# Retention plus mixture-of-experts on one core: sixteen second products for a fifth tile of at most 64 tokens, low rows put together by VectorE and added by a scatter, other orders of y buffers and of GpSimd's gathers

## The chip, the cores and the metric

The kernel runs on one core of a Trainium2 chip. The metric is the device time of one execution in microseconds (us). TensorE (PE) multiplies; its weight loads are listed apart as PEld. VectorE is DVE, ScalarE is ACT, GpSimd is POOL, and SP issues most of the plain transfers.

## The reference, cut to what matters

```
scores = scale * q @ k^T;  ret = scores * D          # D[h,i,j] = gamma_h^(i-j) for i >= j, else 0
x = (ret @ v) as rows of 512 for 4608 tokens          # 8 batches x 576 positions, 8 heads x 64
idx, gate = argmax and softmax weight of the cosine logits of x with 8 expert rows, / tau
for e in range(8):
    mask = idx == e
    h = max(x[mask] @ w1[e], 0)                        # 512 -> 1024
    out[mask] = gate[mask] * (h @ w2[e])               # 1024 -> 512
```

Every token goes to exactly one of eight experts. Sizes are float32 throughout.

## The kernel before, in words

The first 171 us compute the retention, route the tokens and do the first products of expert 0. The rest is a loop over the eight experts (lines 1416 to 1436), and all of the change lies there or in tables built ahead of it. The order of instructions on each engine is the order in which the code is written; no scheduler moves them.

**Slots.** Each expert has CT = 5 tiles of 128 slots. A token of rank r in its expert takes slot r. Within a tile, slots are dealt out so that even ranks lie on partitions 0 to 63 and odd ranks on 64 to 127 (`route_onehot`, line 294), so the first 64 tokens of a tile fill partitions 0 to 31 and 64 to 95. The tables `gid` (token to read, 0 for an empty slot) and `sid` (row to write, a number beyond the bounds for an empty slot) have one column for each tile. `left` holds for each expert how many tokens lie beyond four tiles, at least 0 (`count_left`, line 487), and PE reads it into registers as `rest[e]`.

**First products** (`product`, line 1210): 28 steps for each expert from 1 on, in the order of `ORDER`, of six matrix products each. They use a seven-product scheme over halves, in which the number of moving columns is 320, 304 or 288 by `rest[e]` (over 96, over 64, the rest). After each step, `follow` has ACT copy a bank into one of the five buffers `ys` (line 1249), DVE add another bank to it (line 1245), and ACT and DVE write the two parts of the hidden rows, `hs[:, 0]` (high) and `hs[:, 1]` (low remainder), at lines 1194 and 1187. `ya`, `yb` and `yc` are the buffers; `yb` for i = 0 to 3 is `ys` 2, 3, 4, 2.

**Second products** (`mm2`, line 1291): for each of the five tiles 24 matrix products of 128 slots by 512 columns of w2: high hs with high w2, high hs with low w2, low hs with high w2, for eight slices of F. ACT scales the bank by the gate into `ys[i]` (line 1315), and POOL issues a scatter of its rows to `out` (line 1277). For the fifth tile of experts 1 to 6 PE jumps over the 24 products when `rest[e]` is 0 (line 1300).

**Tasks.** Between these, `run_tasks` writes the preparation of the next expert into the engines' streams: `mm2_plan` has numbered places 3i + k for part k of tile i, `mm1_plan` one place for each of the 28 steps. `gather` (POOL) fetches the rows of a tile; `xturn` (ACT copy at line 404, then a transposing transfer on SP) turns them, `xjoin`, `xsums`, `xhigh`, `xlow` split them; `w1sum`, `w1hi`, `w1lo` split w1; `gather_gates` (POOL) fetches gate values. In `mm2_plan(e)` these prepare expert e + 1, with gathers for e + 2; `w1lo` of w1 part 1 is the last thing of place 9.

Lines 1299 to 1309 hold the second products, cut:

```
last = i == CT - 1 and 0 < e < NE - 1
with tc.If(rest[e] > 0) if last else nullcontext():
    for j, f in enumerate(SECOND):
        for k, (hsp, ws) in enumerate(((0, 0), (0, 1), (1, 0))):
            nc.tensor.matmul(ps[:, :step], hs[:, hsp, f, i * P : (i + 1) * P], w[:, ws, f, n : n + step], ...)
```

## Time and profile before

| what | us |
|---|---|
| median of 3 runs (lowest, highest) | 560.64 (558.1, 561.66) |
| the profiled execution's own time | 554.6 |
| its span, first to last instruction | 552.8 |
| retention, routing and first products of expert 0 | 171.8 |
| second products of the eight experts, first to last | 171.8 to 548 |
| second products of expert 2 / 3 / 4 | 27.2 / 27.2 / 22.3 |

The profiled execution is 6 us shorter than the median of the timed runs. A sum over its rows is therefore made against 554.6 us, and a difference is then taken over to the median. In the rows further down, times are us from the span's start; a bracket behind a row is the idle time of the engine just before it and what ended it.

### The profile page before, as it was taken

How to read it: one execution, taken by the hardware profiler on the slowest of the kernel's cores; microseconds unless marked ns; L12 is line 12 of the kernel's file. 1: busy time of each engine (PE TensorE's matmuls, PEld its weight loads, DVE VectorE, ACT ScalarE, POOL GpSimd, SP SyncE). 2: the span in 40 equal slices, each digit the busy share in tenths (PEclk: the TensorE clock that was granted, in tenths of full speed). 3: DMA queues.
4: the chain of work that ended last, by engine and by line, in shares of the span. 5: the costliest groups of instructions: out<-in, count | busy, mean ns of one | idle time of the engine just before them, and what ended most of it. 6: DMA issues, size and time to landing. Idle time of an engine off the chain costs nothing. (4 is left out here: it accounts for less than half of the span.)

```text
span 552.8 us, 13528 instructions
## 1 busy us (share of the span) xinstructions
PE 544.5 (98%) x5067; PEld 491.3 (89%) x5067; DVE 417.2 (75%) x939; ACT 375.8 (68%) x700; POOL 240.2 (43%) x233
## 2 busy tenths in 40 slices
PE   8999999999999999999999999999999999999996
PEld 8898988898898899889988988998898899889986
DVE  4856778789875967986896789589978948976810
ACT  1256454457767959967895898589879858957511
POOL 6674435543463661265056207603730750343022
PEclk9999999999999999999999999999999999999999
DMA  9999999968459555847765765557567558641211
GB/s 316 390 392 377 376 319 357 377 254 287 149 195 195 169 184 135 170 145 171 156 179 169 148 154 172 171 158 156 177 172 154 171 173 149 159 133 54 77 39 50
DMA packets 81109, 109.57 MB, mean 198 GB/s; under 512 B 42327, under 2 KB 43771, under 8 KB 81024
## 3 DMA queue, kind: packets, MB, share of 16 engines
q1 hardware_dynamic: 71920, 86.24, 54.1%
q0 software_dynamic: 7696, 19.95, 10.8%
q10 hardware_dynamic: 1408, 2.17, 1.2%
q8 instruction: 62, 1.02, 0.8%
q14 instruction: 23, 0.19, 0.1%
HBM read 80.27 MB, written 19.94 MB: 181 GB/s over the span
## 5 line engine op out<-in xcount | busy, mean ns | idle before, releaser
L1303 PE MATMUL m<-w2s,hs 128*128 128x512 f32 x600 | 138.1, 389 | 0.0
L1303 PEld LDWEIGHTS m<-w2s,hs 128*128 128x128 f32 x600 | 112.4, 188 | 23.2
L1277 POOL DMA_INDIRECT out<-y,sid x41 | 50.3, 1227 | 178.9 <-DVE raw L422 122.7
L1303 PE MATMUL a<-w2s,hs 128*128 128x512 f32 (+1 forms) x360 | 78.8, 375 | 0.0
L1303 PEld LDWEIGHTS a<-w2s,hs 128*128 128x128 f32 x360 | 64.2, 188 | 11.9
L363 POOL DMA_INDIRECT raw<-xd,gid x40 | 44.0, 1101 | 29.4 <-ACT xsb L446 11.8
L376 POOL DMA_INDIRECT gt<-gd,gid x40 | 43.9, 1098 | 19.1 <-issue 12.0
L1187 DVE SCALAR_TENSOR_TENSOR hs<-y,hs 128x320 fp32r<-128x320 f32 x84 | 43.8, 528 | 7.6 <-ACT hs L1194 5.6
L411 ACT COPY raw<-raw 128x1024 uint16<-128x1024 uint16 x35 | 47.9, 1367 | 0.8 <-DMA raw<-raw 0.8
L1194 ACT ACTIVATE hs<-y 128x320 fp32r<-128x320 f32 x84 | 39.4, 476 | 12.6 <-DVE y L1245 11.8
L705 POOL TENSOR_TENSOR kt<-kt,cs 128x512 f32<-128x512 f32 x28 | 28.3, 1042 | 44.9 <-DMA kt<-kn 44.9
L1245 DVE TENSOR_TENSOR y<-a,y 128x320 f32<-128x320 f32 x53 | 25.4, 485 | 29.6 <-ACT y L1249 29.2
L1122 DVE TENSOR_TENSOR w2s<-raw,w2s 128x1024 fp32r<-128x1024 f32 x32 | 39.1, 1221 | 8.4 <-ACT w2s L1119 8.3
L1225 PE MATMUL m<-xsb,w0s 128*128 128x288 f32 (+2 forms) x270 | 43.6, 300 | 0.2
L1225 PE MATMUL a<-xsb,w0s 128*128 128x288 f32 (+2 forms) x270 | 43.2, 300 | 0.0
L1315 ACT ACTIVATE y<-m,gt 128x512 f32<-128x512 f32 x26 | 18.0, 691 | 34.3 <-PE m L1303 34.3
L1225 PEld LDWEIGHTS m<-xsb,w0s 128*128 128x128 f32 x270 | 38.8, 188 | 0.6 <-ACT y L1249 0.6
L1225 PEld LDWEIGHTS a<-xsb,w0s 128*128 128x128 f32 x270 | 38.9, 188 | 0.1
L404 ACT COPY raw<-raw 128x1024 uint16<-128x1024 uint16 x35 | 36.7, 1048 | 0.0
L1119 ACT CAST w2s<-raw 128x1024 fp32r<-128x1024 f32 x32 | 33.4, 1043 | 2.9 <-DMA raw<-w 2.9
L724 POOL TENSOR_TENSOR qkt<-qkt,gsb 128x384 f32<-128x384 f32 x32 | 31.3, 1005 | 5.6 <-issue 3.4
L450 DVE TENSOR_TENSOR xsb<-raw,xsb 128x128 fp32r<-128x128 f32 x70 | 30.5, 483 | 0.0
(259 smaller groups left out, 1177.9 us busy)
## 6 DMA issues: line engine op xcount, KB each, us to landing
raw<-w SPq DMA_DIRECT2D x64, 512.0 KB, 4.0
qkt<-qk SPq DMA_DIRECT2D x28, 576.0 KB, 7.4
xd<-y SPq DMA_DIRECT2D x36, 256.0 KB, 9.4
vt<-vs SPq DMA_DIRECT2D x7, 1152.0 KB, 13.0
kt<-kn SPq DMA_DIRECT2D x7, 1024.0 KB, 10.5
qkt<-qk ACTq DMA_DIRECT2D x4, 288.0 KB, 5.5
qkt<-qk SPq DMA_DIRECT2D x4, 288.0 KB, 5.5
out<-y,sid POOLq DMA_INDIRECT x41, 3.4
```

Source lines behind the costliest of these rows:

```text
L363: nc.gpsimd.indirect_dma_start(out=t[:, XO : XO + DM], out_offset=None, in_=xd[:rows, :], in_offset=bass.IndirectOffsetOnAxis(ap=gid[:, a ...
L376: nc.gpsimd.indirect_dma_start(out=g[:, i : i + 1], out_offset=None, in_=gd[:, :], in_offset=bass.IndirectOffsetOnAxis(ap=gid[:, a : a + 1 ...
L404: nc.scalar.copy(far.rearrange("p (h n) -> p h n", h=2), near.rearrange("p (n h) -> p h n", h=2))
L411: nc.scalar.copy(far.bitcast(U16).rearrange("p (n h) -> p h n", h=2), near.rearrange("p (h n) -> p h n", h=2))
L724: nc.gpsimd.tensor_tensor(out=q, in0=q, in1=gsb[:, p, :], op=ALU.mult)
L1119: nc.scalar.copy(hi, u)
L1122: nc.vector.tensor_tensor(out=lo, in0=u, in1=hi.bitcast(F32), op=ALU.subtract)
L1187: nc.vector.scalar_tensor_tensor(out=lo, in0=part(src), scalar=0.0, in1=hi.bitcast(F32), op0=ALU.max, op1=ALU.subtract)
L1194: nc.scalar.activation(hi, part(src), AF.Relu)
L1225: nc.tensor.matmul(ps[:, :n_cols], w[:, ws, ka, d * P : (d + 1) * P], xop(kx, xsp)[:, d, :n_cols], start=(n in (1, 2, 5) and d == 0 and k ...
L1277: put = nc.gpsimd.indirect_dma_start(out=out.rearrange("t (k n) -> (t k) n", k=k), out_offset=bass.IndirectOffsetOnAxis(ap=rows, axis=0), ...
L1303: nc.tensor.matmul(ps[:, :step], hs[:, hsp, f, i * P : (i + 1) * P], w[:, ws, f, n : n + step], start=(j == 0 and k == 0), stop=(j == NF - ...
```

## The change

For the fifth tile of experts 1 to 6 PE now has three ways: 24 products as before when `rest[e]` is over 64, 16 products when it is 1 to 64, none when it is 0. The 16 products use a tile `ht` in which the high rows of the tile's first 64 slots and their low rows stand beside each other as 128 rows: partitions of the product 0 to 31 and 64 to 95 are high, 32 to 63 and 96 to 127 low. With w2 high and w2 low as the two moving operands they give two rows of y for each token.

`both_parts` has DVE put `ht` together with four copies of 128 x 256 elements out of `hs`, into two pieces of `w0s` that held nothing; it stands in place 9 of `mm2_plan`, for every expert from 1 to 6, whatever its count. The first scatter writes the high rows as before. `add_low` issues a second scatter of the same buffer, `ys[4]`, that adds the low rows to them; it is written after step 10 of the next expert's first products and waits for the first scatter. Its rows come from `sidx`, and the gates of the fifth tile from `gidx`; `low_rows` computes both tables once, with 11 small DVE instructions, and `count_left` one more (`few`). When `few` is 0 for an expert, `sidx` holds rows beyond the bounds.

Moved besides: `xturn(n, 0)` goes from step 8 of the first products to place 12 of the second products before them; `gather` of tiles 2 and 3 goes one place later; `gather_gates` goes in three calls in place of four; `yb` for i = 0 to 3 is `ys` 2, 3, 2, 4.

The diff, cut:

```diff
@@ gather_gates
+            ids = gidx[:, e : e + 1] if fitted(e, i) else gid[:, a : a + 1]
-                in_offset=bass.IndirectOffsetOnAxis(ap=gid[:, a : a + 1], axis=0),
+                in_offset=bass.IndirectOffsetOnAxis(ap=ids, axis=0),
...
+    def low_rows():
+        q = P // 4
+        g, r = tab[:, 0, :NE], tab[:, 1, :NE]
+        nc.vector.memset(r, BIG)
+        nc.vector.tensor_copy(g, fifth(gid))
+        for k in (0, 2):
+            to, of = slice((k + 1) * q, (k + 2) * q), slice(k * q, (k + 1) * q)
+            nc.vector.tensor_copy(g[to], fifth(gid)[of])
+            nc.vector.tensor_copy(r[to], fifth(sid)[of])
...
+        ht = [w0s[:, o : o + NPR * P].rearrange("p (f c) -> p f c", f=NPR) for o in (28 * P, 4096 + 28 * P)]
...
-            ya, yb, yc = ys[min(i, 1)], ys[2 + i % 3], ys[0]
+            ya, yb, yc = ys[min(i, 1)], ys[(2, 3, 2, 4)[i]], ys[0]
...
+        def both_parts():
+            for k in range(2):
+                for o, v in enumerate(ht):
+                    t = hs[:, k, NPR * o : NPR * (o + 1), (CT - 1) * P :].rearrange("p f (h c) -> p f h c", h=2)
+                    v = v.rearrange("p f (h s c) -> p f h s c", h=2, s=2)
+                    nc.vector.tensor_copy(v[:, :, :, k, :], t[:, :, :, : HB // 2])
+        def add_low(e):
+            put_rows(ys[CT - 1], 1, sidx[:, e : e + 1], firsts[e])
...
+                if fitted(e, i):
+                    with tc.If(rest[e] > HB) as many:
+                        passes(three)
+                    with many.Else():
+                        with tc.If(rest[e] > 0):
+                            passes(((ht, 0), (ht, 1)))
...
-                    plan[(2, 4, 7, 8, 11)[i]].append((gather, n + 1, i))
-            for k, a0, a1 in ((2, 0, 2), (5, 2, 3), (8, 3, 4), (11, 4, CT)):
+                    plan[(2, 4, 8, 9, 11)[i]].append((gather, n + 1, i))
+            if fitted(e, CT - 1):
+                plan[9].insert(1, (both_parts,))
+            for k, a0, a1 in ((2, 0, 2), (5, 2, 4), (9, 4, CT)):
                 plan[k].insert(0, (gather_gates, n, a0, a1))
+            if n + 1 < NE:
+                plan[12].append((xturn, n + 1, 0))
...
-                plan[8] = [(xturn, n, 0)]
...
+                    if k == 10 and fitted(e - 1, CT - 1):
+                        add_low(e - 1)
```

What this does to three engines follows, in rows of the order in which instructions stand (line numbers are each kernel's own; `waits` names the engines or queues whose semaphores the instruction waits for).

PE at the end of the second products of expert 2, from the fourth tile on; `m_69` and `m_68` are banks. Before:

```order
L1303 MATMUL m_69<-w2s,hs 128x512 x24
L1300 COMPARE_AND_BRANCH
L1303 MATMUL m_68<-w2s,hs 128x512 x24
L1300 UNCONDITIONAL_BRANCH
L1300 UNCONDITIONAL_BRANCH [waits PE_49]
L1234 COMPARE_AND_BRANCH
```

And now:

```order
L1349 MATMUL m_69<-w2s,hs 128x512 x24
L1366 COMPARE_AND_BRANCH
L1349 MATMUL m_68<-w2s,hs 128x512 x24
L1366 UNCONDITIONAL_BRANCH
L1369 COMPARE_AND_BRANCH
L1349 MATMUL m_68<-w2s,w0s 128x512 [waits DVE_49]
L1349 MATMUL m_68<-w2s,w0s 128x512
L1349 MATMUL m_68<-w2s,w0s 128x512 [waits DVE_49]
L1349 MATMUL m_68<-w2s,w0s 128x512 x13
L1369 UNCONDITIONAL_BRANCH
L1369 UNCONDITIONAL_BRANCH [waits PE_49]
L1264 COMPARE_AND_BRANCH
```

The way of 16 products waits for DVE twice, at its first and its third product; the way of none keeps its wait for PE's own work.

DVE in the second products of expert 2, around the end of place 9; `raw_82` holds the rows of tile 4 of expert 3, `wsum` sums of w1. Before:

```order
L450 TENSOR_TENSOR xsb<-raw_82,xsb 128x2x64 [waits Activation_49]
L450 TENSOR_TENSOR xsb<-raw_82,xsb 128x4x2x64 [waits Activation_49]
L1122 TENSOR_TENSOR wsa<-wsum,wsa 128x1024 [waits Activation_49]
L1145 TENSOR_TENSOR wsum<-raw_83 128x256 [waits DMAHW0_49,DVE_49]
L1145 TENSOR_TENSOR wsum<-raw_83 128x256
```

And now:

```order
L454 TENSOR_TENSOR xsb<-raw_82,xsb 128x2x64 [waits Activation_49]
L454 TENSOR_TENSOR xsb<-raw_82,xsb 128x4x2x64 [waits Activation_49]
L1331 COPY w0s<-hs 128x8x32 x4
L1152 TENSOR_TENSOR wsa<-wsum,wsa 128x1024 [waits Activation_49]
L1366 UNCONDITIONAL_BRANCH
```

The four copies stand behind all of the split of x and ahead of the split of w1.

ACT from the last two tiles of the second products of expert 1 to step 9 of the first products of expert 2; `raw_78` holds the rows of tile 0 of expert 3, and `y_84` to `y_88` are the five buffers `ys`. Before:

```order
L1119 CAST wsa<-raw_83 128x768 [waits DMAHW3_49]
L1315 ACTIVATE y_88<-a_64,gt 128x512 [waits DMASW3_49,PE_49]
L1249 COPY y_84<-a_66 128x320 [waits DMASW6_49,PE_49]
...
L1249 COPY y_84<-a_66 128x320 [waits PE_49,Activation_49]
L404 COPY raw_78<-raw_78 128x1024 [waits DMASW1_49]
L1234 UNCONDITIONAL_BRANCH x2
L1249 COPY y_87<-a_65 128x320 [waits DMASW1_49,PE_49]
```

And now:

```order
L1149 CAST wsa<-raw_83 128x768 [waits DMAHW3_49]
L408 COPY raw_78<-raw_78 128x1024 [waits DMASW1_49]
L1375 ACTIVATE y_88<-a_64,gt 128x512 [waits PE_49]
L1279 COPY y_84<-a_66 128x320 [waits DMASW6_49,PE_49]
...
L1279 COPY y_84<-a_66 128x320 [waits PE_49,Activation_49]
L1279 COPY y_87<-a_65 128x320 [waits DMASW2_49,PE_49]
```

The copy of `xturn` leaves the stretch of first products and stands ahead of the scaling of the fifth tile.

## Rows read from the trace of the kernel before

**Rows 1.** The page: busy us (share) xinstructions; granted clock in 40 slices.

```profile
PE 544.5 (98%) x5067; PEld 491.3 (89%) x5067; DVE 417.2 (75%) x939; ACT 375.8 (68%) x700; POOL 240.2 (43%) x233
PEclk9999999999999999999999999999999999999999
```

**Rows 2.** Timeline of PE: start, us, line, operands, shape, count [idle before].

```profile
199.02 1.86 PE L1225 MATMUL a<-xsa,wsa 128*128 128x304 f32 x12
...
249.58 1.76 PE L1225 MATMUL a<-xsa,w0s 128*128 128x288 f32 x12
...
272.22 11.07 PE L1303 MATMUL a<-w2s,hs 128*128 128x512 f32 x48
283.13 16.48 PE L1303 MATMUL m<-w2s,hs 128*128 128x512 f32 x72
299.45 1.76 PE L1225 MATMUL a<-xsa,w0s 128*128 128x288 f32 x12
...
349.32 1.75 PE L1225 MATMUL a<-xsa,wsa 128*128 128x288 f32 x12
...
388.26 5.60 PE L1303 MATMUL m<-w2s,hs 128*128 128x512 f32 x24
394.18 2.02 PE L1225 MATMUL a<-xsa,w0s 128*128 128x320 f32 x12 [0.32 <-PEq L1300]
```

**Rows 3.** Busy time by stretch: stretch, length, then PE, PEld, DVE, ACT, POOL, clock.

```profile
249.58:272.22 22.64, 22.59 (x170) 22.29 (x168) 16.80 (x28) 19.21 (x36) 7.09 (x7) 1.00 0.70 159
272.22:299.45 27.23, 27.23 (x123) 22.54 (x121) 23.66 (x55) 21.39 (x35) 14.00 (x12) 1.00 0.67 162
```

**Rows 4.** Waits of PE's weight loads: us in total, times, longest.

```profile
PEld m L1225 <- ACT y L1249: 1.3, 4, 0.4
```

**Rows 5.** Timeline of DVE in the second products of expert 2.

```profile
277.96 0.29 DVE L429 TENSOR_TENSOR raw<-raw 128x128 f32<-128x128 f32 x1
278.17 0.42 DVE L450 TENSOR_TENSOR xsa<-raw,xsa 128x256 fp32r<-128x256 f32 x1
278.50 0.75 DVE L1145 TENSOR_TENSOR wsum<-raw 128x256 f32<-128x256 f32 x2
...
293.62 1.21 DVE L1122 TENSOR_TENSOR wsa<-wsum,wsa 128x1024 fp32r<-128x1024 f32 x1
...
301.30 0.49 DVE L1245 TENSOR_TENSOR y<-a,y 128x320 f32<-128x320 f32 x1 [3.95 <-ACT y L1249]
```

**Rows 6.** Timeline of ACT in the first products of expert 2.

```profile
256.52 1.05 ACT L404 COPY raw<-raw 128x1024 uint16<-128x1024 uint16 x1
...
260.46 0.45 ACT L1249 COPY y<-a 128x320 f32<-128x320 f32 x1
...
261.48 0.47 ACT L1194 ACTIVATE hs<-y 128x320 fp32r<-128x320 f32 x1 [0.19 <-DVE y L1245]
...
264.42 0.42 ACT L1249 COPY y<-m 128x320 f32<-128x320 f32 x1
```

**Rows 7.** Timeline of ACT: end of expert 2's second products; first products of expert 5.

```profile
294.80 0.82 ACT L1119 CAST w0s<-raw 128x768 fp32r<-128x768 f32 x1
299.65 0.69 ACT L1315 ACTIVATE y<-m,gt 128x512 f32<-128x512 f32 x1 [4.03 <-PE m L1303]
...
403.86 0.43 ACT L1249 COPY y<-m 128x320 f32<-128x320 f32 x1 [0.92 <-DMA out<-y,sid]
```

**Rows 8.** Timeline of DVE around line 491, at the end of expert 0's first products.

```profile
173.66 0.16 DVE L491 TENSOR_SCALAR left<-a 128x8 int32<-128x8 f32 x1
174.54 0.42 DVE L1167 SCALAR_TENSOR_TENSOR hs<-m,hs 128x256 fp32r<-128x256 f32 x1 [0.72 <-ACT hs L1166]
176.72 0.43 DVE L422 TENSOR_TENSOR raw<-raw 128x256 f32<-128x256 f32 x1 [1.76 <-ACT raw L411]
```

**Rows 9.** POOL's timeline in expert 3's first products; scatters of line 1277, issue to landing.

```profile
308.84 0.88 POOL L1145 TENSOR_TENSOR wsum<-raw,wsum 128x256 f32<-128x256 f32 x1
...
DMA to landing us min/median/max: 2.2/3.4/6.1
```

More of the change, by code (lines that the diff above doesn't have):

```diff
@@ L358, in retention_moe, with fitted @@
     BEG = group_tiles(B - 3)[0] * P
+    def fitted(e, i):
+        return i == CT - 1 and 0 < e < NE - 1
     def gather(e, i, rows=N):
@@ L484, in retention_moe, with fifth @@
     left = keep.tile([P, NE], I32, name="left")
+    few = tab[:, 0, NE : 2 * NE]
+    gidx = keep.tile([P, NE], I32, name="gidx")
+    sidx = keep.tile([P, NE], I32, name="sidx")
     rest = []
+    def fifth(t):
+        return t.rearrange("p (e i) -> p e i", i=CT)[:, :, CT - 1]
+    def low_rows():
[7 more added lines that the diff above has]
+            nc.vector.tensor_copy(r[to], fifth(sid)[of])
+        nc.vector.tensor_tensor(out=g, in0=g, in1=fifth(gid), op=ALU.subtract)
+        nc.vector.tensor_tensor(out=g, in0=g, in1=few, op=ALU.mult)
+        nc.vector.tensor_tensor(out=gidx, in0=g, in1=fifth(gid), op=ALU.add)
+        nc.vector.scalar_tensor_tensor(out=r, in0=r, scalar=-BIG, in1=few, op0=ALU.add, op1=ALU.mult)
+        nc.vector.tensor_scalar(out=sidx, in0=r, scalar1=BIG, scalar2=None, op0=ALU.add)
     def count_left():
@@ L1274, in retention_moe, with put_rows @@
         puts = []
-        def put_rows(rows_of_y, k, rows):
+        firsts = {}
+        def put_rows(rows_of_y, k, rows, first=None):
             put = nc.gpsimd.indirect_dma_start(
@@ L1283, in put_rows @@
                 oob_is_err=False,
+                compute_op=ALU.add if first else ALU.bypass,
             )
             for other in puts:
-                tc.declare_no_dep(put.ins, other.ins, reason="a scatter writes other rows or other columns")
+                if other is not first:
+                    tc.declare_no_dep(put.ins, other.ins, reason="a scatter writes other rows or other columns")
             puts.append(put)
+            return put
         last_rows = []
+        def both_parts():
[6 more added lines that the diff above has]
+            put_rows(ys[CT - 1], 1, sidx[:, e : e + 1], firsts[e])
         def mm2(e, i, tasks):
@@ L1298, in mm2, with passes, between @@
                 ps = psm.tile([P, 512], F32, name="m")
-                last = i == CT - 1 and 0 < e < NE - 1
-                with tc.If(rest[e] > 0) if last else nullcontext():
+                def passes(forms, inner=lambda m: None):
+                    m = 0
                     for j, f in enumerate(SECOND):
-                        for k, (hsp, ws) in enumerate(((0, 0), (0, 1), (1, 0))):
+                        for rows, ws in forms:
                             nc.tensor.matmul(
                                 ps[:, :step],
-                                hs[:, hsp, f, i * P : (i + 1) * P],
+                                rows[f // NPR][:, f % NPR] if rows is ht else rows[:, f],
                                 w[:, ws, f, n : n + step],
-                                start=(j == 0 and k == 0),
-                                stop=(j == NF - 1 and k == 2),
-                            )
-                            if not last and step == DM and (3 * j + k) % 8 == 7 and 3 * j + k < 23:
-                                tasks((3 * j + k) // 8)
-                if last:
+                                start=(m == 0),
+                                stop=(m == NF * len(forms) - 1),
+                            )
+                            m += 1
+                            inner(m)
+                def between(m):
+                    if step == DM and m in (8, 16):
+                        tasks(m // 8 - 1)
+                hi, lo = (hs[:, k, :, i * P : (i + 1) * P] for k in range(2))
+                three = ((hi, 0), (hi, 1), (lo, 0))
+                if fitted(e, i):
[4 more added lines that the diff above has]
+                            passes(((ht, 0), (ht, 1)))
                     tasks(0)
                     tasks(1)
+                else:
+                    passes(three, between)
                 nc.scalar.activation(y[:, n : n + step], ps[:, :step], AF.Copy, scale=gts[e][:, i : i + 1])
@@ L1320, in mm2 @@
                 if a < NA - 2:
-                    put_rows(*part)
+                    firsts[e] = put_rows(*part)
                 else:
@@ L1408, in retention_moe @@
             13: [(xturn, 1, 2)],
-            14: [(count_left,), (xturn, 1, 3)],
+            14: [(count_left,), (low_rows,), (xturn, 1, 3)],
         }
```

3 lines of the change are left out of this document (added).

## The prediction

> **What bounds the kernel now.** I read the page first: the line of busy times and the line of the granted clock. [...]
>
> Second, PE's timeline, to see how full it is and which experts the change touches. The second products of expert 2 run from 272.22 to 299.45 without a gap; 48 products take 10.91 us, 0.227 us each, and a tile of 24 takes 5.45. The stage of first products tells the count of each expert by its columns: 288 for experts 2, 3 and 4, which is at most 64 in the fifth tile; 304 or 320 for experts 1, 5, 6 and 7 (rows of expert 1 and 5 stand for them). After expert 4 one group of 24 follows the fourth tile's place directly by first products: four tiles only, so its fifth is jumped over already [rows 2]. **Only experts 2 and 3 can take the way of 16.**
>
> Third, busy time by stretch: in the second products of expert 2 DVE is busy 23.66 of 27.23 us and ACT 21.39, in its first products 16.80 and 19.21 of 22.64 [rows 3]. Fourth, the waits: the only one of PE in the expert loop that repeats is that of its weight loads for ACT's copy of a bank, 1.3 us in four times [rows 4]. Last, the timelines of DVE, ACT and POOL at the places where the change puts something.
>
> **The products.** Two experts save 8 products of 0.227 us: 2 x 1.82 = -3.64 us [rows 2]. Experts 1, 5 and 6 keep 24, expert 4 keeps none.
>
> **The copies for `ht`.** They cover two of the three possible ways for nothing, but on the way of 16 PE waits for them, and they come late. In expert 2 the instruction behind which place 9's split of x ends, and ahead of which the copies now stand, begins at 293.62 [rows 5]; DVE has little idle time before it, and nothing ahead of it in the order is moved. The fifth tile begins at 283.13 + 48 x 0.227 = 294.0 [rows 2]. The first product needs the first and the third copy. No row shows a copy from SBUF to SBUF of this size on DVE. From above I bound it by a TENSOR_TENSOR of 128 x 256, 0.42 us long with the next one 0.33 later; from below by one of 128 x 128, 0.29 long with the next 0.21 later [rows 5]. The third copy then ends at 293.62 + 2 x 0.33 + 0.42 = 294.70, or at 294.33. How long PE takes to start again I read after expert 4: the last group ends at 388.26 + 5.60 = 393.86 and the next product starts at 394.18, 0.32 later [rows 2]. So PE starts the fifth tile at 294.65 to 295.02 in place of 294.0: it waits 0.65 to 1.0 us. The fourth copy is 0.2 to 0.3 behind the third, within the two products that go first. Nothing excludes that DVE comes earlier than in this trace, so the lower end is no wait at all. I take 0.8 in each of two experts: +1.6 us (0 to 2.0). **Almost half of what is saved goes into this wait.**
>
> [...]
>
> What the copies delay: each expert's split of w1, its sums and a second split, by at most 4 x 0.33 = 1.3 us. After them DVE is idle 3.95 us until the first products [rows 5], so this costs nothing while that idle time is there; on the way of 16 the first products come 1 us sooner, which it still covers. After expert 4, where the fifth tile is missing, it is not there, and I come back to that.
>
> **The moved `xturn`.** PE's four waits for ACT [rows 4] come at step 20 in experts 2 to 5: the product accumulates on a bank that ACT still has to copy. In expert 2 that copy runs from 264.42 to 264.84. ACT has been working almost without idle time from the `xturn` copy of step 8 on, at 256.52, 1.05 us long [rows 6]. With it gone ACT runs ahead until something else holds it: the copy at 260.46 reads step 13, which ends on PE at about 249.58 + 13 x 0.793 + 0.16 = 260.05, with a step of 22.2 / 28 us, so 0.4 us are won at that point, and the following wait for DVE at 261.48 hangs on that same copy and moves with it [rows 2, 3, 6]. 0.4 us is the longest of the four waits [rows 4]. I take 1.1 of the 1.3 us back: -1.1 (0 to -1.3). Where the copy goes instead, before the scaling of the fifth tile, ACT is idle 4.03 us [rows 7].
>
> The other order of `yb` gives the copy of step 17 a wait for DVE in place of one for a scatter. DVE's low part of that buffer is written after step 14, three steps of 0.8 us earlier; costed at nothing. Without that cover the wait would come back at step 20, which is a rival below.
>
> **Expert 5** follows a stage of four tiles. ACT there waits 0.92 us for a scatter to leave `ys` [rows 7], which the other order of gathers brings forward; against that stand the copies' 1.3 us on DVE and the `xturn` copy ahead of the first step. I set them off against each other. A second compare on the way of none: +0.1.
>
> **POOL and the adding scatter.** Six scatters more, each about 1 us of POOL. POOL's last work in the first products of expert 3 ends at 309.72, so the adding one is issued by about 311; landing takes 3.4 us in the median and 6.1 at most [rows 9], so it is down by 314.4 to 317.1. It is waited for by ACT's copy of step 21, ready at 299.45 + 21 x 0.793 = 316.1, and PE needs that copy two steps later. Nothing to 0.3 us; I take nothing. Only experts 2 and 3 add rows.
>
> **`low_rows`.** Twelve small DVE instructions of 0.16 us at least, say 2 us, behind the one at 173.66; 0.72 and 1.76 us of idle time follow at once, and PE has begun tile 0 of the second products, which doesn't read what is late [rows 8]. Nothing.
>
> **Sum:** -3.64 + 1.6 - 1.1 + 0.1 = -3.0 us; 554.6 becomes 551.6 in a profiled execution. The median of the timed runs lies 6 us above that execution; the difference carried over gives 560.6 - 3.0 = **557.6 us**, 0.5% less. About 1% is what a measurement of this kernel can tell from no change. By the terms' own ends the likeliest case runs from 560.6 - 3.64 - 1.3 = 555.7 to 560.6 - 3.64 + 2.0 + 0.1 = 559.1.
>
> **Rivals.**
> - *No wait for the copies.* DVE reaches them a microsecond sooner, or they are short, and all stalls go: -3.64 - 1.3 = -4.9, 555.7 us. For it: ACT is relieved ahead of the stage. Against it: DVE's stream in the second products starts from ACT's join of tile 0, which doesn't move. Chance 0.15.
> - *The jumps cost.* The ways of 24 and of 16 now both end or begin with a jump over code that is not used. [...] As a mechanism of this kernel: the one long jump of before, after expert 4, shows 0.48 us from the end of the stream of products (388.26 + 24 x 0.227 = 393.70 to 394.18) [rows 2]. Five more such would be +2.4: 560.0 us. Against it: that jump waits for PE's own work, which the new ones don't, and in every step with 288 columns PE jumps over the code for 320 and 304, with 22.59 of 22.64 us busy over 28 steps [rows 3]. Chance 0.10.
> - *ACT stays behind.* The stalls at step 20 stay, by the new wait for DVE or by expert 5: 558.7 us. Chance 0.12.
> - *The adding scatter is slow, and the kernel gets slower.* Place: ACT's copy of step 21 in the first products of experts 3 and 4, with all of ACT's work behind it, then PE at step 24. Landing is covered up to about 6 us, and from 7.5 us on the gain of 3.0 is gone (1.5 in each of two experts); at 12 us, twice the longest seen [rows 9], it costs 2 x 6 = 12, and 557.6 becomes 569.6 us. No row shows a scatter that adds. Chance 0.06.
> - *The change doesn't do what it says:* if neither expert took the way of 16, what is left is -1.1 + 0.1: 559.6. The columns of experts 2 and 3 speak against it. Chance 0.02.
>
> **Chances and range.** The forecast has 0.55. All cases but the slow scatter lie between 555.7 and 560.0; timed runs of one kernel lie 2.5 us below and 1 above their median, which I add at both ends for the range: 554.0 to 561.2. Faster by over 1% is below 555.0, which only the best case with a low measurement reaches: 0.12. Slower by over 1% is above 566.2, the slow scatter or several costs of ACT: 0.07. Within 1%: 0.81.
>
> **What would show it.** PE in experts 2 and 3: 16 products in the fifth tile, a gap of 0.6 to 1.0 us ahead of the first of them that is put down to DVE's copy, second products of 26.2 us in place of 27.2. No such gap in experts 1, 5, 6. PE's wait for ACT's copies near 0 in place of 1.3. DVE idle about 2.6 us ahead of the first products in place of 3.95. ACT's copy of step 21 without idle time put down to a scatter. I am wrong if the copies are done by the time the fourth tile ends, if PE shows gaps behind the 24 products, or if the adding scatter holds ACT.

## The result, and the profile after

| what | before | after |
|---|---|---|
| median, us (lowest to highest, runs) | 559.7 (557.3 to 561.66, 6) | **551.47** (550.78 to 552.98, 6) |
| the profiled execution's own time, us | 554.6 | 551.17 |
| its span, us | 552.8 | 549.1 |

The ratio is 0.9855 [0.9829, 0.9881]: the changed kernel is 1.5% faster, 8.2 us where 3.0 were forecast, and lies below the range that I gave. The two profiled executions differ by only 3.4 us (3.7 in span). So the first question is why the medians differ by 8.2 and the profiles by 3.4.

What the profiles show comes first. The page of after, to be read against [rows 1]:

```profile
span 549.1 us, 13547 instructions
PE 541.6 (99%) x5051; PEld 489.4 (89%) x5051; DVE 419.9 (76%) x975; ACT 377.4 (69%) x700; POOL 250.9 (46%) x239
PEclk9999999999999999999999999999999999999999
```

PE has 16 products fewer, DVE 36 instructions more, POOL 6. PE stays the bound, busy 99% with no other engine above 76%: what shortens its stream shortens the time, and work put on another engine costs only where PE comes to wait for it. PE's timeline of after at the end of expert 2's second products, and behind the four tiles of expert 4 (columns as in [rows 2]):

```profile
281.70 11.04 PE L1349 MATMUL m<-w2s,hs 128*128 128x512 f32 x48
292.95 4.00 PE L1349 MATMUL m<-w2s,w0s 128*128 128x512 f32 x16 [0.21 <-DVE w0s L1331]
296.79 1.76 PE L1255 MATMUL a<-xsa,w0s 128*128 128x288 f32 x12
...
390.05 2.03 PE L1255 MATMUL a<-xsa,w0s 128*128 128x320 f32 x12 [0.32 <-PEq L1369]
```

The fifth tile is 16 products, it waits for DVE's copies, and the next stage comes at 296.79. Busy time of after by stretch, first and second products of expert 2 (columns as in [rows 3]):

```profile
248.44:270.80 22.36, 22.36 (x170) 22.35 (x168) 16.42 (x28) 18.51 (x35) 6.46 (x7) 1.00 0.67 162
270.80:296.79 25.99, 25.78 (x114) 20.95 (x113) 24.51 (x59) 22.33 (x36) 14.18 (x13) 1.00 0.54 160
```

22.36 stands against 22.64, and 25.99 against 27.23. DVE's timeline of after at that place, then the group of the copies (duration in ns: shortest, median, longest):

```profile
290.60 1.69 DVE L454 TENSOR_TENSOR xsb<-raw,xsb 128x128 fp32r<-128x128 f32 x4
292.21 1.05 DVE L1331 CAST w0s<-hs 128x256 fp32r<-128x256 f32 x4
293.18 1.21 DVE L1152 TENSOR_TENSOR wsa<-wsum,wsa 128x1024 fp32r<-128x1024 f32 x1
...
298.64 0.49 DVE L1275 TENSOR_TENSOR y<-a,y 128x320 f32<-128x320 f32 x1 [1.80 <-ACT y L1279]
```

```profile
L1331 DVE CAST w0s<-hs x24: 282/288/443, 242.0 to 487.4; 128x256 fp32r<-128x256 f32 x24
```

DVE still idles 1.80 us ahead of the first products, so what the copies delay is covered. Stage lengths, from the starts of PE's rows (us; "start" is where e0's second products begin; the last four rows belong to the experiments):

| kernel | start | first products e1, e2, e3, e4, e5 | second e2, e3 | span |
|---|---|---|---|---|
| before | 171.76 | 23.36, 22.64, 22.65, 22.60, 25.12 | 27.23, 27.22 | 552.8 |
| after | 170.62 | 23.39, 22.36, 22.73, 22.31, 25.20 | 25.99, 25.94 | 549.1 |
| before_again | 170.51 | 23.73, 24.33, 24.57, 23.43, 25.15 | 27.21, 27.23 | 556.5 |
| moves_only | 171.30 | 23.36, 22.35, 22.27, 22.21, 25.47 | 27.2, 27.2 | 551.6 |
| sixteen_only | 170.73 | 24.43, 25.91, 22.67, 24.09, 26.61 | 25.98, 26.00 | 557.0 |
| after_again | 171.06 | 23.39, 22.36, 22.34, 22.30, 24.76 | 25.96, 25.92 | 548.6 |

The start lies between 170.3 and 173.2 in all traces; the change has no part there, so 1.1 us of the 3.7 are scatter of the early part. Against after_again, which has no extra wait in expert 3, the loop gives 1.25 us in the first products of experts 2 to 5 and 2.57 in the two second products, less 0.3 elsewhere: **3.5 us, where the sum said 3.0.** The mechanism and its size were right; what failed is how the profile was carried over to the timed runs. The line "before_again" shows where to look: the same program as before, in an execution of 558.26 us, loses 4.8 us in the first products of experts 1 to 4.

### The profile page after: what moved, and what is told of

Its sections match the earlier page's. It is cut to its first block, busy times and chain, and to the rows that moved or that the text cites. A ratio compares the mean times of both kernels' runs of the same rounds, so it can differ in the third digit from the quotient of the medians.

```text
span 549.1 us, 13547 instructions
## 1 busy us (share of the span) xinstructions
PE 541.6 (99%) x5051; PEld 489.4 (89%) x5051; DVE 419.9 (76%) x975; ACT 377.4 (69%) x700; POOL 250.9 (46%) x239
## 5 line engine op out<-in xcount | busy, mean ns | idle before, releaser
L1349 PE MATMUL m<-w2s,hs 128*128 128x512 f32 x552 | 127.2, 389 | 0.0
L1349 PEld LDWEIGHTS m<-w2s,hs 128*128 128x128 f32 x552 | 103.4, 188 | 21.3
L1309 POOL DMA_INDIRECT out<-y,sid x41 | 45.7, 1115 | 166.1 <-ACT y L1375 134.1
L366 POOL DMA_INDIRECT raw<-xd,gid x40 | 42.9, 1073 | 19.4 <-issue 9.3
L380 POOL DMA_INDIRECT gt<-gd,gid x34 | 39.0, 1146 | 17.2 <-issue 9.7
L1217 DVE SCALAR_TENSOR_TENSOR hs<-y,hs 128x320 fp32r<-128x320 f32 x84 | 42.3, 510 | 3.3 <-ACT hs L1224 1.3
```

Source lines behind the costliest of these rows:

```text
L366: nc.gpsimd.indirect_dma_start(out=t[:, XO : XO + DM], out_offset=None, in_=xd[:rows, :], in_offset=bass.IndirectOffsetOnAxis(ap=gid[:, a ...
L380: nc.gpsimd.indirect_dma_start(out=g[:, i : i + 1], out_offset=None, in_=gd[:, :], in_offset=bass.IndirectOffsetOnAxis(ap=ids, axis=0),)
L1217: nc.vector.scalar_tensor_tensor(out=lo, in0=part(src), scalar=0.0, in1=hi.bitcast(F32), op0=ALU.max, op1=ALU.subtract)
L1309: put = nc.gpsimd.indirect_dma_start(out=out.rearrange("t (k n) -> (t k) n", k=k), out_offset=bass.IndirectOffsetOnAxis(ap=rows, axis=0), ...
L1349: nc.tensor.matmul(ps[:, :step], rows[f // NPR][:, f % NPR] if rows is ht else rows[:, f], w[:, ws, f, n : n + step], start=(m == 0), stop ...
```

## Experiments

Five groups of runs were made, each on one chip with its own runs of the kernel before. The median of before was 558.2 us in the first group, 554.9 in the second and third, 555.1 in the fourth and 559.1 in the fifth; the second and the fifth ran on the same chip. This spread is itself a finding, so kernels are compared within a group. Three theories were set against each other first: M (PE's waits for ACT and DVE in the expert loop make up the 6 us, and the moved orders take them away), S (the extra time lies ahead of expert 1) and A (it comes from the recording alone).

### First group: halves of the change

**before_again**: the kernel before, unchanged.

> The kernel before, unchanged. Open is why its timed runs (557.3 to 561.7 us) are 3 to 7 us longer than its one profiled execution (554.6 us), while the changed kernel's timed runs (550.8 to 553.0) lie at its own profiled one (551.2). Theory M (waits that come and go): the extra time stands in the expert loop, in waits of ACT and POOL that the profiled execution of before happened not to have; then a new profiled execution near 558 us has its extra 3 to 5 us behind 171.8 us, where the second products of expert 0 start. Theory S (early stage): the extra time stands ahead of the expert loop, which the change's instructions do not touch; then second products of expert 0 start at 174 to 177 us. Theory A (accident): the new profiled execution again takes 554 to 555 and the timed ones 557 to 562, so recording is what differs. Time expected by all three: 557 to 562, ratio 1.00.

Measured: 558.27, ratio 0.9998 [0.9976, 1.0021]. PE's waits in its trace, in total, times and longest (weight loads twice, then products), where [rows 4] had 1.3 us in four times:

```profile
PEld a L1225 <- ACT y L1249: 3.6, 4, 1.5
PEld m L1225 <- ACT y L1249: 2.4, 5, 0.7
```

```profile
PE a L1225 <- ACT y L1249: 2.6, 3, 1.3
```

**moves_only**: before with the four orders of the change.

```diff
-ya, yb, yc = ys[min(i, 1)], ys[2 + i % 3], ys[0]
+ya, yb, yc = ys[min(i, 1)], ys[(2, 3, 2, 4)[i]], ys[0]
-plan[(2, 4, 7, 8, 11)[i]].append((gather, n + 1, i))          # gathers
+plan[(2, 4, 8, 9, 11)[i]].append((gather, n + 1, i))
-for k, a0, a1 in ((2, 0, 2), (5, 2, 3), (8, 3, 4), (11, 4, CT)):   # gates
+for k, a0, a1 in ((2, 0, 2), (5, 2, 4), (9, 4, CT)):
+plan[12].append((xturn, n + 1, 0))        # and no longer at step 8 of the first products
```

> The kernel before with the four other orders alone: y buffers of the join (2, 3, 2, 4), gathers of the next expert's rows at places 2, 4, 8, 9, 11, gates at 2, 5, 9, the xturn of tile 0 at place 12 of the second products. All fifth tiles keep 24 products, no adding scatter. Theory M: most of the gain that was not forecast is here, 560 - 1.1 - 4.8 = 554 us (553 to 555.5). Theory S: the stalls of step 20 alone go, 560 - 1.1 = 559 us (558 to 560).

Measured: 553.63, ratio 0.9921 [0.9891, 0.9951], 4.4 us [2.7, 6.1] less.

**sixteen_only**: after, with gathers, gates and `xturn` put back; `yb` stays as in after.

```diff
-plan[(2, 4, 8, 9, 11)[i]].append((gather, n + 1, i))
+plan[(2, 4, 7, 8, 11)[i]].append((gather, n + 1, i))
-for k, a0, a1 in ((2, 0, 2), (5, 2, 4), (9, 4, CT)):
+for k, a0, a1 in ((2, 0, 2), (5, 2, 3), (8, 3, 4), (11, 4, CT)):
-plan[12].append((xturn, n + 1, 0))
+plan[8] = [(xturn, n, 0)]                 # in the first products, as before
```

> The changed kernel with three of the orders put back: gathers at 2, 4, 7, 8, 11, gates at 2, 5, 8, 11, xturn of tile 0 at step 8 of the first products; the 16 products, the copies, the adding scatter and the order of y buffers stay. By the stages of the two profiled executions the 16 products are worth 1.24 + 1.28 = 2.5 us. Theory M: 560 - 2.5 = 557.5 us (556.5 to 559). Theory S, where something else in the changed program (its place in memory, its new small tiles) shortens the early stage: 551.5 + 1.1 = 552.6 us (551.5 to 554).

Measured: 558.09, ratio 0.9996 [0.9967, 1.0026]. Its second products have the 2.5 us (25.98 and 26.00), but its first products lose 1.1, 3.3, 1.5 and 1.5 us in experts 1, 2, 4 and 5.

**after_again**: the changed kernel once more.

> The changed kernel, unchanged, beside the three others on one chip. All theories: 551 to 553.5 us, ratio 0.983 to 0.988. If the gain belonged to the chip that the first comparison ran on, it would be 556 to 557 here beside 560 for before.

Measured: 550.98, ratio 0.9873 [0.9844, 0.9903].

So M holds in this group, and S and A of the first meaning fall: the start is no later, and a recorded execution takes 558.26 us where A expected 554 to 555. Two recorded executions of the same kernel differ inside the loop. What happens there is seen in expert 2. First PE and ACT of before_again, whose stage starts at 248.74:

```profile
251.13 0.96 PE L1225 MATMUL a<-xsa,w0s 128*128 128x288 f32 x6
251.94 0.95 PE L1225 MATMUL a<-xsb,w0s 128*128 128x288 f32 x6
252.73 0.96 PE L1225 MATMUL m<-xsa,w0s 128*128 128x288 f32 x6
253.53 0.96 PE L1225 MATMUL m<-xsb,w0s 128*128 128x288 f32 x6
255.56 1.19 PE L1225 MATMUL a<-xsb,w0s 128*128 128x288 f32 x7 [1.08 <-ACT y L1249]
```

```profile
251.24 0.47 ACT L1194 ACTIVATE hs<-y 128x320 fp32r<-128x320 f32 x1
254.30 0.42 ACT L1249 COPY y<-a 128x320 f32<-128x320 f32 x1 [2.59 <-PE m L1225]
255.09 0.42 ACT L1249 COPY y<-a 128x320 f32<-128x320 f32 x1 [0.36 <-PE m L1225]
```

Then the same product and the same copy in moves_only, whose stage starts at 249.12:

```profile
251.51 0.96 PE L1225 MATMUL a<-xsa,w0s 128*128 128x288 f32 x6
```

```profile
252.51 0.43 ACT L1249 COPY y<-a 128x320 f32<-128x320 f32 x1 [0.54 <-PE a L1225]
```

In moves_only ACT's copy starts 0.04 us behind the end of the product that it reads (252.47). In before_again that product ends at 252.09 and the copy starts at 254.30, 2.21 us later, with ACT idle; PE goes on at its pace until it needs the bank, and then waits. I call this a late signal. POOL's timelines there, of before_again and of moves_only:

```profile
250.24 0.97 POOL L376 DMA_INDIRECT gt<-gd,gid  x1 [0.30 <-issue]
251.51 1.69 POOL L363 DMA_INDIRECT raw<-xd,gid  x1 [0.30 <-issue]
253.51 1.01 POOL L1277 DMA_INDIRECT out<-y,sid  x1 [0.30 <-issue]
```

```profile
248.02 0.97 POOL L363 DMA_INDIRECT raw<-xd,gid  x1 [0.31 <-issue]
250.28 1.00 POOL L1277 DMA_INDIRECT out<-y,sid  x1 [1.29 <-ACT y L1315]
```

In before_again POOL issues indirect transfers without a break (0.30 us between two) until 5.78 us into the stage, and signals are late until 6.43; in moves_only the run is broken by a wait for ACT. In this trace of before the signals are late until 0.6 to 1.3 us past the end of POOL's run in experts 1 to 4 and in 6 (runs until 4.56, 5.78, 5.78, 4.51, 3.36 us; late until 5.34, 6.43, 6.66, 5.26, 4.63), and not in expert 7, where POOL has a lone scatter. In expert 5, where the run lasts until 9.78, single signals are late until 10.29, ACT's copies by up to 0.72 us, without loss. **In the profiled execution of before that the prediction read, no signal is late**, although POOL's run is about as long there (until 4.51 to 4.57 us in experts 1 to 4).

The profiled execution of after, which is one of the six timed ones of the first comparison (551.17 us), does have late signals, in experts 1 to 5. In expert 5 the product of step 4 ends at 394.73 and ACT is free from 395.08 (PE, then ACT):

```profile
393.69 1.04 PE L1255 MATMUL a<-xsb,w0s 128*128 128x320 f32 x6
```

```profile
396.19 0.43 ACT L1279 COPY y<-a 128x320 f32<-128x320 f32 x1 [1.11 <-PE m L1255]
```

So the two profiles of the first comparison are not alike: after's has late signals, which cost it little, and before's has none.

### Second to fourth group: which of the orders

From here the rivals are H, held signals (PE's signals come late while POOL's run of indirect transfers reaches into the first products, so an order that shortens the run helps), and A, now with another meaning: ACT's load, relieved by the moved `xturn`.

**gathers_only** (before with the lines marked "gathers" and "gates" above), **xturn_only** (before with the `xturn` line), **pool_dose** (moves_only with two more indirect transfers on POOL behind step 1 of each first products, whose rows nothing reads):

```diff
+spare = keep.tile([P, 2 * NE], F32, name="spare")
+def two_more(e):
+    for k in range(2):
+        nc.gpsimd.indirect_dma_start(out=spare[:, 2 * e + k : 2 * e + k + 1], out_offset=None, in_=gd[:, :],
+            in_offset=bass.IndirectOffsetOnAxis(ap=gid[:, e * CT + k : e * CT + k + 1], axis=0))
+1: [(two_more, e)],
```

**gates_first** (after, with `((0, 0, CT),)` as the one call of `gather_gates`).

> The kernel before with GpSimd's order alone changed: gathers of rows at places 2, 4, 8, 9, 11, gates at 2, 5, 9. Read from the last traces: in the slower executions PE's signals to ACT and DVE come up to 2.2 us late in the first steps of the first products (ACT's copy of step 4 of expert 2 starts at 254.30, its product ended at 251.93), and go back to normal 0.6 to 1.3 us after POOL's last indirect DMA of the tail (ends 3.4 to 6.0 us into the stage with the old order, 2.2 with the new). Theory H (held signals): the length of POOL's tail decides; 558.2 - 3.5 = 554.7 us (554 to 555.5), what is left to the moved kernel (553.6) being the stalls of step 20. Theory A (ACT's load: what the xturn copy at step 8 does to ACT decides): 557 to 558.2.

> The kernel before with the xturn of tile 0 alone moved from step 8 of the first products to place 12 of the second. Theory H: POOL's tail keeps its length, the stalls behind step 4 stay, only those of step 20 go: 557.1 us (556.3 to 558). Theory A: 553.6 to 555.

> The kernel with the four other orders alone, and two more indirect DMAs of POOL in each expert's first products, behind step 1: each gathers one gate a row into a tile that nothing reads. They bring no load to PE, ACT or DVE and 1 KB of data in all. POOL's tail ends about 2.5 us later, at 4.7 us into the stage. Theory H: the stalls come back without the old orders, 553.6 + 3 = 556.6 us (555.5 to 558.5), PE's signals late until 5 to 6 us into the stage. Theory A: 553.6 us (553.2 to 554.2), no stall.

> The changed kernel with all five gathers of gates at place 0 of the second products in place of 2, 5 and 9. POOL reaches them as soon as the adding scatter is issued, so about 12 to 19 us into the first products, and its tail at the start of the next first products is shorter by about three of 1.27 us. Theory H: PE's signals come on time at the start of the stage and late in the steps from 14 to 23; 551.0 us if ACT has the time there (550 to 552), 553 to 555 if it doesn't. Theory A: 551.0 us.

Measured: 554.84 (0.9988 [0.9969, 1.0007]); 556.15 (1.0025 [1.0011, 1.0038]); 554.61 (0.999 [0.9976, 1.0004]); 552.0 (0.9945 [0.9925, 0.9964]). This tells H from A in nothing, because the effect is absent: before takes 554.9 here, and no trace of this group has a late signal. Only one of the parts costs something in this group: xturn_only loses 3.3 us in expert 5, where ACT's copy waits for a scatter that still reads its buffer, and PE for the copy (timelines of ACT and of PE):

```profile
405.72 0.43 ACT L1249 COPY y<-m 128x320 f32<-128x320 f32 x1 [4.41 <-DMA out<-y,sid]
```

```profile
406.20 1.22 PE L1225 MATMUL m<-xsb,w0s 128*128 128x320 f32 x6 [1.89 <-ACT y L1249]
407.22 1.80 PE L1225 MATMUL m<-xsa,wsa 128*128 128x320 f32 x6
```

After this wait six products take 1.80 us in place of about 1.04: the clock is granted at half for 3.41 us, and the page's row of it has an 8 in that slice and a 9 in all others.

The same kernels beside after on other chips, to find the effect again:

> The changed kernel, unchanged, once more beside the three others. On the chip of the last four runs (chip 13) the kernel before took 554.9 us and none of PE's signals was late; on the chip of the four before them (chip 5) it took 558.2 and they were late in six of seven first-product stages. Theory H (held signals): on a chip that holds PE's signals before takes 557 to 560 and the change is worth 6.5 to 8 us (551 to 552); on one that doesn't, before takes 554.5 to 555.5 and the change is worth what its products and the stalls of step 20 are, 3 us (551.5 to 552.5). Theory A (ACT's load): the same share on every chip, 0.987.

> The kernel before with the four other orders alone. Theory H: 553.5 to 554.5 on either kind of chip, since its POOL tail is too short to be held for long: 4 to 5 us under before where signals are held, 0.5 to 1 us where not. Theory A: ratio 0.992 on either.

> The same with two more indirect DMAs of POOL behind step 1 of each expert's first products (each gathers one gate a row into a tile that nothing reads). Theory H: on a chip that holds signals 2 to 4 us over the kernel with the four orders alone, the signals late until 5 to 6 us into the stage; on a chip that doesn't, within 0.5 us of it. Theory A: within 0.5 us of it on either.

> The kernel before with GpSimd's order of gathers and gates alone changed. On chip 13 it took what before took (554.84 beside 554.91). Theory H: on a chip that holds signals 554.5 to 556, most of the gain of the four orders, and nothing on one that doesn't. Theory A: nothing on either.

Measured: after 550.55, 0.9934 [0.9912, 0.9955]; moves 553.95, 0.9985 [0.997, 1.0]; dose 554.75, 1.0 [0.9982, 1.0019]; gathers 554.84, 0.9994 [0.9979, 1.0009]. No signal is late here either. **Without late signals the whole change is worth 3.7 us [2.5, 4.9] and the orders 0.8 [0, 1.7]**: the sum of the prediction, in a group in which the timed runs of before agree with the execution that I read (554.88 and 554.6).

The fourth group repeated two of them and added **copies_early**, which tests the wait for the copies: after, with the four copies a little earlier in DVE's order.

```diff
-plan[9].insert(1, (both_parts,))
+plan[9].insert(0, (both_parts,))
```

> The four other orders and two more indirect DMAs of POOL behind step 1 of each expert's first products (each gathers one gate a row into a tile that nothing reads). On a chip where before takes 557 to 560: theory H 556 to 559, PE's signals late until 5 to 6 us into the stage; theory A 553.6 to 554.3, as the four orders alone took there (553.6). On a chip where before takes 555: 554.7 by both, as twice before.

> The kernel before with GpSimd's order of gathers and gates alone changed. On a chip where before takes 557 to 560: theory H 554.5 to 556; theory A 557 to 560. On a chip where before takes 555: 554.8 by both.

> The changed kernel with the four copies ahead of the last split of x of place 9 in place of behind it, some 0.85 us of DVE earlier. In the changed kernel PE starts the 16 products 0.35 us after the fourth tile's end, put down to the copies. If that is their lateness, the gap goes to under 0.05 us in experts 2 and 3 and the time falls by 0.6 to 0.7 us: 549.9 to 550.4 beside 550.6 to 551.0. If it is the jump between the ways, the gap stays, 550.6 to 551.0.

Measured: dose 555.06 (0.9985 [0.9963, 1.0007]), gathers 554.63 (0.9974 [0.9951, 0.9997]), copies_early 550.86 (0.9903 [0.9871, 0.9934]). PE's timeline of copies_early at the same place as in after:

```profile
284.21 11.05 PE L1349 MATMUL m<-w2s,hs 128*128 128x512 f32 x48
295.10 3.89 PE L1349 MATMUL m<-w2s,w0s 128*128 128x512 f32 x16
298.83 1.36 PE L1255 MATMUL a<-xsa,w0s 128*128 128x288 f32 x9
```

The gap ahead of the 16 products is gone, and both second products take 25.53 us, 0.4 less than after. The gap in after was the wait for the copies, and nothing else. The time, 550.86, is not in the 549.9 to 550.4 expected for that. Whether copies_early beats after in the timed runs can't be told: 550.86 and 551.47, 550.98, 550.55 were never measured side by side, and 0.9 us in two stages is less than the groups tell apart.

### Fifth group: with late signals again

> The four other orders and two more indirect DMAs of POOL behind step 1 of each expert's first products (each gathers one gate a row into a tile that nothing reads). On a chip where before takes 557 to 560: theory H 556 to 559, theory A 553.6 to 554.3. On a chip where before takes 555: 554.8 by both, as three times before.

> The kernel before with GpSimd's order of gathers and gates alone changed. On a chip where before takes 557 to 560: theory H 554.5 to 556, theory A 557 to 560. On a chip where before takes 555: 554.8 by both, as three times before.

> The kernel before with the xturn of tile 0 alone moved from step 8 of the first products to place 12 of the second. On a chip where before takes 557 to 560: theory H 556.5 to 559, theory A 553.6 to 555. On a chip where before takes 555: 556.1 by both, 1.2 us over before, as on chip 13, where the stage of expert 5 took 3.3 us more with ACT waiting for a scatter.

Here before took 559.08, on the chip on which it had taken 554.9. Measured: dose_fifth 562.19, 1.0049 [1.0015, 1.0083]; gathers_fifth 558.09, 0.9978 [0.996, 0.9995]; xturn_fifth 561.97, 1.0051 [1.003, 1.0072]. Each of the three programs has a trace with and one without late signals, and the difference of the spans lies in the first products:

| program | span, without | span, with | where it is longer |
|---|---|---|---|
| before | 552.8 | 556.5 | e1 0.37, e2 1.69, e3 1.92, e4 0.83 |
| moves_only + two transfers | 552.9 | 557.9 | e1 1.99, e3 0.33, e5 3.05 |
| gathers_only | 553.3 | 557.3 | e5 4.15 |
| xturn_only | 555.4 | 560.1 | e1 0.89, e2 1.06, e3 1.69, e4 1.44 |

In the first row the start is 1.25 us earlier with late signals, which makes up the rest; in the last, expert 5 is 0.44 shorter. The added transfers in expert 1 show the effect of POOL's run. PE, ACT and POOL of dose_fifth, whose stage starts at 198.27:

```profile
201.63 0.99 PE L1236 MATMUL a<-xsb,wsa 128*128 128x304 f32 x6
...
205.86 1.10 PE L1236 MATMUL a<-xsb,wsa 128*128 128x304 f32 x6 [1.56 <-ACT y L1260]
```

```profile
205.05 0.43 ACT L1260 COPY y<-m 128x320 f32<-128x320 f32 x1 [1.91 <-PE a L1236]
```

```profile
201.34 0.98 POOL L489 DMA_INDIRECT spare<-gd,gid  x1 [0.30 <-issue]
202.62 1.97 POOL L489 DMA_INDIRECT spare<-gd,gid  x1 [0.30 <-issue]
```

ACT and POOL of dose_third, the same program in the third group, whose stage starts at 197.46:

```profile
201.02 0.43 ACT L1260 COPY y<-m 128x320 f32<-128x320 f32 x1 [0.62 <-PE m L1236]
```

```profile
202.28 0.94 POOL L489 DMA_INDIRECT spare<-gd,gid  x1 [0.31 <-issue]
```

The copy comes 3.56 us into the stage there and 6.78 in dose_fifth. POOL's run ends 5.8 us into the stage in dose_third and 6.3 in dose_fifth. In dose_fifth signals are late until 7.0 us and PE waits 1.56 us; in dose_third a run of nearly the same length costs nothing. In experts 2 to 4, where a wait for ACT breaks POOL's run, the same two transfers cost little in dose_fifth either (22.36, 22.68, 22.35, against 22.36, 22.35, 22.30 in pool_dose).

gathers_fifth loses nothing in the four stages of experts 1 to 4, as H expected. Signals are late there too, but only early in the stage: in experts 2 to 4 POOL's run ends 0.06 to 0.41 us into the stage, signals are late until 1.4 to 1.6, and PE doesn't wait for them. ACT's scaling of the fifth tile in expert 2, 1.31 us into the stage of gathers_fifth (which starts at 250.29) and 0.20 into that of gathers_only (250.45):

```profile
251.60 0.69 ACT L1315 ACTIVATE y<-a,gt 128x512 f32<-128x512 f32 x1 [5.14 <-PE a L1225]
```

```profile
250.65 0.69 ACT L1315 ACTIVATE y<-a,gt 128x512 f32<-128x512 f32 x1 [4.03 <-PE a L1303]
```

But gathers_fifth was to take 554.5 to 556 by H, and took 558.09: expert 5 takes it back. There POOL's run starts behind only four tiles and lasts 6.9 us into the stage (POOL, then ACT):

```profile
399.32 1.22 POOL L363 DMA_INDIRECT raw<-xd,gid  x1 [0.30 <-DVE w2s L1122]
400.84 1.00 POOL L1277 DMA_INDIRECT out<-y,sid  x1 [0.30 <-issue]
```

```profile
402.91 0.42 ACT L1249 COPY y<-m 128x320 f32<-128x320 f32 x1 [4.24 <-remote]
```

A is refuted: by it the dose was to take 553.6 to 554.3, as moves_only had in the first group, and the `xturn` move alone to bring most of the gain, and both came out slower than before. H comes nearer, but all three times lie above its ranges: 562.19 against 556 to 559 for the dose, 558.09 against 554.5 to 556 for the gathers, 561.97 against 556.5 to 559 for `xturn`.

H is not the whole cause. In sixteen_only's expert 3 POOL's run lasts until 7.75 us and signals are late only until 3.5; in after_again's expert 3 it lasts until 4.5 us and copies come only some 0.3 us late, with no loss. And the same run costs nothing in the second to fourth group. **In the stages above signals are late until at most 1.5 us past POOL's last indirect transfer (gathers_fifth, experts 2 to 4), so POOL's run bears on how long; it doesn't bring late signals by itself. What holds the signals, and why in one group of runs and not in another on the same chip, stays open.**

## Why the prediction was right or wrong, point by point

- **The bound, and who takes the way of 16.** Right: PE stays the bound, and experts 2 and 3 alone take that way, 16 products each.
- **The products**, -3.64: together with the wait for the copies they gave -1.24 and -1.28 in after, -2.52; the sum had -3.64 + 1.6 = -2.04.
- **The copies**, +1.6: here a term was mis-sized. Their start was forecast at 293.62; less 1.42 us, by which expert 2's second products start earlier in after (270.80 against 272.22), that is 292.20, and it is 292.21. Their length is at the lower of my two bounds: 0.29 us, four in 1.05. The fifth tile was due at 281.70 + 48 x 0.227 = 292.60 and began at 292.95: **0.35 us of wait in place of 0.65 to 1.0**. What was too much is the 0.32 us that I added for PE to start again, read behind a jump after expert 4 [rows 2]: the third copy runs from 292.61 to 292.90, and PE starts 0.05 later. By that row the allowance belonged to the jump, not to the wait. Some 0.1 to 0.2 us behind the 16 products stays: 292.95 + 16 x 0.227 = 296.58, and the next stage comes at 296.79; in copies_early 295.10 + 3.63 = 298.73, and 298.83.
- **What the copies delay.** Covered, as forecast: DVE's idle time ahead of the first products goes from 3.95 to 1.80 us (2.6 were forecast) and is not used up.
- **The moved `xturn`**, -1.1: the four waits of 1.3 us [rows 4] are one of 0.4 in after, and none of the four stages keeps its stall in after_again: -1.25 us there. The move alone, without late signals, is seen in xturn_only: 22.27, 22.27 and 22.22 us in experts 2 to 4 against 22.64, 22.65 and 22.60, -1.1 in three stages; what it does in expert 5 follows.

```profile
PEld a L1255 <- ACT y L1279: 0.4, 1, 0.4
```

- **Expert 5**, set to nothing: 25.20 and 24.76 against 25.12. The two effects that I set off against each other are real and large. The move of `xturn` alone is bad there (28.41 in xturn_only, 27.97 in xturn_fifth). The move of the gathers alone is good without late signals (24.72 in gathers_only) and bad with them (28.87 in gathers_fifth). The changed kernel has both moves.
- **POOL and the adding scatter**, at nothing: right. Issue is longer than the 1 us that I took, 1.61; from issue to landing the six take 2.7 to 5.1 us in after_third, 3.8 in the median, close to [rows 9]. From after_third, the group of the six (ns shortest, median, longest):

```profile
L1309 POOL DMA_INDIRECT out<-y,sidx x6: 1597/1608/2397, 259.7 to 504.5; - x6
```

- **`low_rows`**, at nothing: the second products of expert 0, behind it, take 27.21 us against 27.26.
- **The rivals.** *No wait for the copies* doesn't hold in after, and holds in copies_early, by an edit. *The jumps cost*: the second products of experts 1, 5 and 6, which keep 24 products, take 27.22, 27.24 and 27.23, so nothing; and the jump over all products after expert 4 shows 0.32 us as before. *ACT stays behind*, *the adding scatter is slow* and *the change doesn't do what it says*: refuted.
- **The step that failed** is "The median of the timed runs lies 6 us above that execution; the difference carried over". I took the 6 us as something that lies outside the program's work and stays; and the other orders of gathers and gates had no term in my sum outside expert 5. In before_again, an execution of 558.26 us, such a surplus lies in the expert loop: 4.8 us of waits for late signals in the first products. A profile without late signals can't show that the change meets them, and the four changed orders (of `yb`, gathers, gates and `xturn`) together take away most: moves_only gains 4.4 us where signals are late and 0.8 where they are not. By the third group's 3.7 us for the whole change without late signals, about 8.2 - 3.7 = 4.5 us of the first result come from the late signals, an estimate across groups (by the first group's 558.2 - 551.0 it would be 7.2 - 3.7 = 3.5). That the timed runs of before in the first comparison had them is concluded from their 557.3 to 561.66 us and from after's trace of that comparison, which has them; traces of those runs of before are not seen. None of my rivals held this case. Nor could a view of the one execution have priced it; that every timed run lay at least 2.7 us above it (557.3 against 554.6) was the one sign, and it called for a rival "the 6 us are waits in the loop, and change with the orders", with the range open below. The range also doesn't follow from its own words: 2.5 below 555.7 and 1 above 560.0 are 553.2 to 561.0, not 554.0 to 561.2. The result lies below both.

The parts don't add up. In the fifth group gathers and gates alone give -1.0 us and `xturn` alone +2.9, in the first the four orders together -4.4. Expert 5 is one place where, with late signals, each of the two needs the other: 28.87 and 27.97 us alone, 25.47 together in moves_only. The `yb` order was not run alone, so what it gives is not shown.

## What to carry to other kernels

Where the timed runs lie well above the profiled execution, the difference is itself work or waiting somewhere; before it is carried over as a constant, several executions are to be compared stage by stage. By these traces, indirect transfers that one engine issues in an unbroken run are best over before a stage in which engines hand banks to each other every 0.8 us, even if one profile shows no cost of them there. And an operand that another engine puts together on the way to a full TensorE is worth a place earlier in that engine's order: it is cheap to move, and the gap goes at once (0.35 us in after, none in copies_early).

## What the runs showed of the hardware that was not expected

- **Late signals.** ACT and DVE see the end of a PE product late, while PE goes on at its normal pace until it needs a bank: ACT by up to 4.2 us (gathers_fifth, expert 5), DVE by up to 5.5 (dose_fifth, expert 5). The signals then come in a burst, 0.07 to 0.08 us apart (in after 0.076 at 398.47, where two of PE's come). It is there in the eight traces of after, of the first and of the fifth group and in none of the twelve others, with before at 558.2 and 559.1 against 554.9 to 555.1. The same eight traces, and only they, also lack about a quarter of the records of landed transfers (3734 to 4045, against 5033 to 5260) and about a tenth of those of the signals of ACT and DVE. The timed executions of the five groups were recorded as well, so the rival that recording brings the late signals is not excluded, and no run here tests it.
- **A gather that takes 3.17 us.** In the first group a gather of expert 3's rows takes 3.17 us in before_again, and ends right behind an instruction of DVE; in before it takes 1.23. POOL and DVE of before_again, then POOL of before at the same place:

```profile
241.59 3.17 POOL L363 DMA_INDIRECT raw<-xd,gid  x1 [2.02 <-ACT xsb L446]
```

```profile
243.96 0.76 DVE L1145 TENSOR_TENSOR wsum<-raw 128x256 f32<-128x256 f32 x2
```

```profile
242.27 1.23 POOL L363 DMA_INDIRECT raw<-xd,gid  x1 [2.02 <-ACT xsb L446]
```

  DVE's row ends at 244.72, the gather at 244.76. In sixteen_only, where the four copies (0.90 us) stand in that run of DVE, the same gather takes 3.98 us. The gather of before_again is 1.9 us longer than that of before; POOL's run ends 1.3 us later (5.78 us into the stage, 4.51 in before), and experts 2 and 3 of before_again, which have such a gather, take 24.3 and 24.6 us against 23.4 in expert 4. That DVE's work holds the gather back is not shown: in before the same rows of DVE stand beside 1.23 us, and it was not tested apart.
- **The clock after a wait.** It was granted at half for 3.41 us in each of three traces, 0.6 to 0.9 us after PE went on from a wait of 1.78 us in sixteen_only, 1.89 in xturn_only and 2.35 in gathers_fifth (there its mean is 0.60 over the first 3.41 us from PE's start on and 0.91 over the 3.87 behind them), but not after 2.16 in dose_fifth or 2.20 in xturn_fifth, where the next six products take 1.04 us, as they do without a wait. That adds to what a late signal costs: in gathers_fifth 2.35 us of wait make 4.15 us of stage.
- **A scatter that adds** holds POOL for 1.61 us, a plain one for 1.02.
